# Feed-forward 2's weight splits moved into feed-forward 1, with DRAM copies; resident loads of w_out one by one; tiles reused in the last rows

## The chip, the cores and the metric

The kernel runs on one core of a Trainium2 chip. The metric is the device time of one execution in microseconds; three runs of the kernel before gave 1107.70, 1107.75 and 1108.04 us, median 1107.75 us.

## The reference, cut to what matters

Three stages follow one another: attention with a cumulative bias, a feed-forward with a cosine (feed-forward 1), and a normalised, gated feed-forward (feed-forward 2). B, H, S, D = 4, 8, 576, 64, so there are 2304 tokens of 512 features.

```python
scores = where(causal, -1e9, q @ k.T / sqrt(D) + minimum(-(cum_i - cum_j), 0))   # cum = cumsum(max(s, 0))
x  = (softmax(scores) @ v)  as [2304, 512]
h  = x @ w_in                     # [512, 2048]
x  = (h * cos(h)) @ w_out         # [2048, 512]
xn = x / sqrt(mean(x * x) + 1e-6) * rms_g
g, val = xn @ w_gate, xn @ w_val  # [512, 1536] each
out = (g * sigmoid(g) * val) @ w_out2        # [1536, 512]
```

The weights reach the chip as 64-bit words. Each product of the feed-forwards is made of three fp32r matmuls: both operands are split into a high part (`[:, 0]`) and a rest (`[:, 1]`), and high times high, high times rest and rest times high are summed in PSUM.

## The kernel before, in words

**A planner sets every order.** `Plan.op` (L90) collects operations with their alternatives (engine, cost in ns), a priority (`plan.now`, a due time) and what they read and write. `Plan.order` (L109) runs a list schedule over the five engines with cost formulas and writes the program in the order of the planned starts. On the chip each engine then works through its own list strictly in that order; what isn't ready holds up all that stands behind it on that engine. All DMAs are issued by SP, in SP's order.

**Weights.** `chunk` (L355) takes one chunk of 128 x 512 weights: a 512 KB DMA into `raw` (three buffers), one operation on ScalarE or GpSimd (`cv`, L361/L362), one on GpSimd (L365), two on VectorE (L366, L368), a copy for the high part (`copy`, L283) and a subtraction for the rest (`two`, L296). The result is a 512 KB tile.

**Feed-forward 1** goes over 9 blocks of 256 tokens, each in 8 ticks (72 ticks, `k = 8 j + m`, L732). A tick takes two chunks of `w_in`: 24 matmuls with 256 columns into a bank `h` (`gemm1`, L634), then a chain: ScalarE L744 (`u`), VectorE L297 (`u` minus `h`), ScalarE L746 (sine), VectorE L297 (times `h`), ScalarE copy L286 (`g`, high part), VectorE L297 (`g`, rest). Then come the 12 matmuls with 512 columns that add `g` times two chunks of `w_out` into the accumulators (`gemm2`, L640), placed behind the next tick's `gemm1`. There are three buffers each of `u` and `g`. The split `w_in` stays in 16 tiles `wi`. The split `w_out` is stored to DRAM as `wo_d`, read back through the 4 tiles `ws` for block 1, and from block 2 (`RES`) on kept in 16 tiles `wr`, which lie where attention's tiles were: `att_end` is the end of all attention operations. Ticks of the first blocks stand between attention's operations.

**Between the blocks** `rms_norm` (L691) copies the accumulators to `y`, squares them on ScalarE, runs 12 tiny VectorE operations and 2 scalings (L713); `rms_store` (L717) transposes on TensorE (L724), copies to `xo` and stores to `xn_d`.

**Feed-forward 2** goes over 6 blocks of 384 tokens, each in 12 units. A unit has 24 matmuls with 384 columns (`gemm1` on a gate and a value chunk) and 9 with 512 (`gemm2` on an output chunk). Its 36 weight chunks are split one after the other (L800 to L806): the first four into `ws`, the rest into `wi` and `wr` as feed-forward 1 gives those tiles back. So from tick 64 on (the last block of feed-forward 1) until unit 10 the splits of 32 chunks run beside the matmuls.

Of the kernel before, what the change touches and what calls it, by code (L numbers as in the profile page):

```python
# [10 lines left out]
F32 = mybir.dt.float32  # L11
# [11 lines left out]
BLK1 = 256  # L23
# [191 lines left out]
def attention_moe_moe(ctx, tc, q2, k2, vp, s, w_in, w_out, w_gate, w_val, w_out2, rms_g, out):  # L215
# [64 lines left out]
    def on(e, ns, fn):  # L280
        return [(e, ns, fn)]
# [20 lines left out]
    def load(o, i, nbytes, r, w, issue=475.0, **kw):  # L302
        return plan.op(on("SP", issue, lambda: sp.dma_start(out=o(), in_=i())), r, w, dma=nbytes, **kw)
# [48 lines left out]
    wo_d = [dbuf(f"wo_d{f}", [128, 2, 512]) for f in range(F1)]  # L352


    def chunk(src, w):  # L355
        raw, g = raw_r.new(), cv_r.new()
        load(raw, lambda: src.bitcast(I32).rearrange("p (c t) -> p c t", t=2), 1 << 19, [], [raw])
        top, low = (lambda: raw()[:, :, 1]), (lambda: raw()[:, :, 0])
        v = lambda: g().bitcast(I32)
        plan.op([  # L360
            ("POOL", pool1(512), lambda: pool.tensor_scalar(out=g(), in0=top().bitcast(F32), scalar1=2.0 ** -112, scalar2=1.0, op0=ALU.mult, op1=ALU.mult)),  # L361
            ("ACT", act_s(512), lambda: act.activation(g(), top().bitcast(F32), AF.Copy, scale=2.0 ** -112)),  # L362
        ], [raw], [g])
# [307 lines left out]
    def tick_at(k):  # L671
        return T_FF1 + k * P_FF1
# [7 lines left out]
        load(wo_d[f], lambda f=f: w2[0, f]().bitcast(F32), 1 << 19, [w2[0, f]], [wo_d[f]])  # L680
    for j in range(1, NB1):
        for f in range(F1):
            if j > RES:
                w2[j, f] = w2[RES, f]
                continue
            plan.now = tick_at(8 * j + f // 2) - 4000.0
            w = w2[j, f] = ws_r.new() if j < RES else wr_r.new(f)
            plan.op(on("SP", 475.0, lambda w=w, f=f: sp.dma_start(out=w().bitcast(F32), in_=wo_d[f]())), [wo_d[f]], [w], dma=1 << 19,
                    after=[att_end] if j == RES else ())

    def rms_norm(j, acc):  # L691
# [24 lines left out]

    def rms_store(j, ys):  # L717
        for k in (0, 2):
            tr, xo = h_bank(j + 1) if j < NB1 - 1 else bank.new(4), xo_r.new()

            def go(tr=tr, k=k):
                for i in range(2):
# [5 lines left out]
            load(lambda k=k: xn_d[j]()[:, k:k + 2, :], lambda xo=xo: xo().rearrange("p (k t) -> p k t", k=2), 1 << 18, [xo], [(xn_d[j], k)])  # L728

    acc = {}  # L730
    xs = {}
    for k in range(8 * NB1):  # L732
        j, m = divmod(k, 8)
        plan.now = tick_at(k) - 12000.0
        if m == 0:
            xs[j] = load_x1(j)
            acc[j] = [psb(f"acc{t}", (t,)) for t in range(2)]
        h, u, g = h_bank(j), u_r.new(), g_r.new()
        for i in range(2):
            plan.now = tick_at(k)  # L740
            w = w1[2 * m + i]
            plan.op(on("PE", 1440, lambda i=i, w=w, h=h, x=xs[j]: gemm1(h()[:, BLK1 * i:BLK1 * i + BLK1], w(), [b() for b in x], BLK1)), [w, *xs[j]], [h])
        plan.now = tick_at(k) - LEAD_E
        plan.op(on("ACT", act_p(512) + 93, lambda u=u, h=h: act.activation(u().bitcast(I32), h(), AF.Identity, bias=quarter)), [h], [u])  # L744
        two(u, lambda u=u: u().bitcast(I32), h, 512, [h], [u], psum=True)
# [14 lines left out]
            plan.now = tick_at(k) - LEAD_E  # L760
            rms_store(j - 1, ys)
    plan.now = tick_at(8 * NB1)
    rms_store(NB1 - 1, rms_norm(NB1 - 1, acc[NB1 - 1]))


    T_FF2 = tick_at(8 * NB1 + 1)
# [132 lines left out]
```

## Time and profile before

| | |
|---|---|
| three runs, median | 1107.75 us |
| the profiled execution | 1110.82 us, its span 1109.0 us |
| TensorE busy | 1080.4 us (97%) |
| VectorE, ScalarE, GpSimd busy | 547.1, 528.7, 187.1 us |
| mean granted TensorE clock | 0.992 |
| the chain that ended last | TensorE 80%, VectorE 9% |

TensorE is busy nearly throughout, so the numbers to look for are the stretches in which it isn't. On the timeline, feed-forward 1 runs alone from about 300 us; tick 64 starts at 587.40 us, and the first matmuls of feed-forward 2 at 640.34 us. PE is TensorE, DVE VectorE, ACT ScalarE, POOL GpSimd, SP the engine that issues DMAs. A matmul's end is modelled, so the pace is read from start to start.

### The profile page before, as it was taken

How to read it: one execution, taken by the hardware profiler on the slowest of the kernel's cores; microseconds unless marked ns; L12 is line 12 of the kernel's file. 1: busy time of each engine (PE TensorE's matmuls, PEld its weight loads, DVE VectorE, ACT ScalarE, POOL GpSimd, SP SyncE). 2: the span in 40 equal slices, each digit the busy share in tenths (PEclk: the TensorE clock that was granted, in tenths of full speed). 3: DMA queues.
4: the chain of work that ended last, by engine and by line, in shares of the span. 5: the costliest groups of instructions: out<-in, count | busy, mean ns of one | idle time of the engine just before them, and what ended most of it. 6: DMA issues, size and time to landing. Idle time of an engine off the chain costs nothing.

```text
span 1109.0 us, 16861 instructions
## 1 busy us (share of the span) xinstructions
PE 1080.4 (97%) x6474; PEld 938.8 (85%) x6474; DVE 547.1 (49%) x1209; ACT 528.7 (48%) x1098; POOL 187.1 (17%) x256
## 2 busy tenths in 40 slices
PE   8899999999999999999999999999999999999998
PEld 5568667777799999999998788999999999999997
DVE  6887998864474543535438888421211211211211
ACT  4889889988754543444435555321211211211111
POOL 3544556321030000000003444100000000000000
PEclk7999999999999999999999999999999999999999
DMA  5765677743392000000002537110000100100000
GB/s 179 239 205 172 212 252 234 241 142 107 123 390 65 22 27 20 20 29 30 20 20 80 164 120 223 39 57 1 25 34 1 57 1 1 43 1 1 30 1 29
DMA packets 51377, 101.28 MB, mean 91 GB/s; under 512 B 7520, under 2 KB 27488, under 8 KB 51296
## 3 DMA queue, kind: packets, MB, share of 16 engines
q1 hardware_dynamic: 51296, 100.19, 27.4%
q8 instruction: 51, 0.84, 0.3%
q14 instruction: 30, 0.25, 0.1%
HBM read 77.63 MB, written 22.54 MB: 90 GB/s over the span
## 4 chain that ended last, share of the span: by engine, by line
PE 80%; DVE 9%; issue 3%; POOL 3%; ACT 3%; DMA 1%; SPq 0%; DVEq 0%; POOLq 0%; ACTq 0%
PE bank L634 40%; PE bank L640 27%; PE bank L500 4%; PE bank L430 3%; PE bank L532 3%; DVE raw L366 2%; DVE cv L368 2%; POOL raw L365 1%; PE bank L457 1%; ACT cv L362 1%; DVE e L485 1%; PE bank L435 1%; DVE u L297 1%; DVE e L442 1%; PE bank L724 1%
## 5 line engine op out<-in xcount | busy, mean ns | idle before, releaser
L640 PE MATMUL bank<-wr,g 128*128 128x512 f32 x996 | 248.5, 396 | 4.7 <-ACT g L286 3.8
L297 DVE TENSOR_TENSOR u<-bank,u 128x512 f32<-128x512 f32 (+1 forms) x144 | 89.8, 623 | 313.0 <-PE bank L634 235.4
L634 PEld LDWEIGHTS bank<-xa,wi 128*128 128x128 f32 x1728 | 215.2, 188 | 9.1 <-DVE u L297 1.6
L634 PE MATMUL bank<-xa,wi 128*128 128x256 f32 x1728 | 221.3, 283 | 1.6 <-DVE u L297 1.4
L640 PEld LDWEIGHTS bank<-wr,g 128*128 128x128 f32 x996 | 182.6, 188 | 43.5 <-ACT g L286 4.9
L286 ACT ACTIVATE g<-u 128x512 fp32r<-128x512 f32 (+1 forms) x130 | 74.8, 576 | 265.2 <-DVE u L297 265.2
L297 DVE TENSOR_TENSOR g<-u,g 128x512 fp32r<-128x512 f32 (+1 forms) x127 | 82.4, 649 | 69.3 <-ACT g L286 69.2
L634 PE MATMUL bank<-xb,wi 128*128 128x384 f32 x528 | 101.8, 338 | 0.0
L634 PEld LDWEIGHTS bank<-xb,wi 128*128 128x128 f32 x528 | 93.7, 188 | 1.6
L634 PE MATMUL bank<-xb,wr 128*128 128x384 f32 x480 | 92.0, 335 | 0.0
L744 ACT ACTIVATE u<-bank,quarter 128x512 int32<-128x512 f32 x72 | 49.2, 684 | 81.0 <-PE bank L634 79.5
L297 DVE TENSOR_TENSOR u<-u,bank 128x512 f32<-128x512 int32 x72 | 49.3, 685 | 77.7 <-ACT u L744 76.2
L634 PEld LDWEIGHTS bank<-xb,wr 128*128 128x128 f32 x480 | 84.6, 188 | 1.8
L469 ACT ACTIVATE e<-e,mn 128x128 f32<-128x128 f32 (+3 forms) x128 | 70.6, 554 | 13.3 <-DVE mn L442 12.5
L746 ACT ACTIVATE u<-u,half_pi 128x512 f32<-128x512 f32 x72 | 52.1, 724 | 41.1 <-DVE u L297 40.8
L442 DVE CUSTOM_DVE_ANT_0 e<-bank,cm 128x128 f32<-128x128 f32 (+3 forms) x128 | 56.9, 484 | 22.9 <-PE bank L435 22.2
L640 PE MATMUL bank<-wi,g 128*128 128x512 f32 x270 | 66.8, 392 | 0.7 <-ACT g L286 0.7
L293 POOL TENSOR_SCALAR g<-u 128x512 fp32r<-128x512 f32 (+1 forms) x14 | 9.2, 659 | 340.6 <-DVE u L297 340.6
L826 ACT ACTIVATE u<-bank 128x384 f32<-128x384 f32 x72 | 35.2, 489 | 64.6 <-PE bank L634 53.2
L361 POOL TENSOR_SCALAR cv<-raw 128x512 f32<-128x512 f32 x20 | 15.0, 751 | 291.8 <-DVE wi L297 252.7
L640 PE MATMUL bank<-ws,g 128*128 128x512 f32 x246 | 64.0, 401 | 0.0
L365 POOL TENSOR_SCALAR raw<-raw 128x512 f32<-128x512 f32 x68 | 52.3, 770 | 68.0 <-ACT cv L362 65.6
(131 smaller groups left out, 1522.8 us busy)
## 6 DMA issues: line engine op xcount, KB each, us to landing
raw<-in_w_out_dram SPq DMA_DIRECT2D x28, 512.0 KB, 3.9
raw<-in_w_in_dram SPq DMA_DIRECT2D x16, 512.0 KB, 4.7
wo_d<-ws SPq DMA_DIRECT2D x16, 512.0 KB, 4.8
ws<-wo_d SPq DMA_DIRECT2D x16, 512.0 KB, 4.1
wr<-wo_d SPq DMA_DIRECT2D x16, 512.0 KB, 10.2
raw<-in_w_val_dram SPq DMA_DIRECT2D x12, 512.0 KB, 3.7
raw<-in_w_gate_dram SPq DMA_DIRECT2D x12, 512.0 KB, 3.7
qr<-in_q_dram SPq DMA_DIRECT2D x16, 320.0 KB, 4.8
```

The lines of the kernel that those rows point to most:

```text
L286: alts.append(("ACT", (act_p if psum else act_s)(n), lambda: act.activation(o(), i(), AF.Copy, scale=scale)))
L297: alts = on("DVE", dve1(n), lambda: dve.tensor_tensor(out=o(), in0=a(), in1=b(), op=op))
L365: plan.op(on("POOL", pool1(512), lambda: pool.tensor_scalar(out=top().bitcast(F32), in0=top().bitcast(F32), scalar1=0.0, scalar2=1.0, op0= ...
L430: pe.matmul(Sp[e]()[:, o:o + w], run.q()[hd, q0:q0 + 128], run.k()[hd, :w], start=(t == ts[0]), stop=False)
L442: plan.op(on("DVE", dve1(w) + 17, lambda o=o, w=w, i=i, e=e: dve.tensor_tensor_reduce(out=Es[e]()[:, o:o + w], in0=Sp[e]()[:, o:o + w], in ...
L469: plan.op(on("ACT", act_s(w) + 187, lambda E=E, o=o, w=w, i=i: act.activation(E()[:, o:o + w], E()[:, o:o + w], AF.Exp, scale=-1.0, bias=s ...
L500: pe.transpose(tr()[:m, 128 * j:128 * j + 128], E[0]()[:, E[2] + c:E[2] + c + m], ident)
L634: pe.matmul(h, w[:, a, 128 * k:128 * k + 128], x[k // 2][:, k % 2, c, :blk], start=(n == 0), stop=(n == 11))
L640: pe.matmul(acc[t], g[a][:, 128 * t:128 * t + 128], w[:, c, :], start=(first and (a, c) == (0, 0)), stop=(last and (a, c) == (1, 0)))
L744: plan.op(on("ACT", act_p(512) + 93, lambda u=u, h=h: act.activation(u().bitcast(I32), h(), AF.Identity, bias=quarter)), [h], [u])
L746: plan.op(on("ACT", act_s(512) + 93, lambda u=u: act.activation(u(), u(), AF.Sin, scale=-TWO_PI, bias=half_pi)), [], [u], table="sin")
L826: plan.op(on("ACT", act_p(BLK2), lambda us=us, h=hs[0]: act.activation(us(), h()[:, :BLK2], AF.Silu)), [hs[0]], [u], table="silu")
```

## The change

1. The 36 chunks of feed-forward 2's weights are split into the 4 `ws` tiles during ticks 24 to 64 of feed-forward 1: chunk n's raw load waits for the end of tick 24 + 40 n / 36. The first 32 are then stored to DRAM (`w3_d0` to `w3_d31`) and, where the split stood before, read back into the `wi` and `wr` tiles. The last four stay in `ws`.
2. The 16 loads of the resident `w_out` copies each wait, besides `att_end`, for the tick four ticks ahead of the one that uses them.
3. The normalisation of the last block gets a due time 20,000 ns later (`RMS_LATE`); the second half of each `rms_store` goes through `ys[0]` instead of `xo`; block 0 of feed-forward 2 uses four banks for `h` instead of five.

```diff
+RMS_LATE = 20000.0
+W3_FROM, W3_TO = 24, 64
-    def chunk(src, w):
+    def chunk(src, w, after=()):
-        load(raw, ..., 1 << 19, [], [raw])
+        load(raw, ..., 1 << 19, [], [raw], after=after)
     for j in range(1, NB1):
         for f in range(F1):
-            if j > RES:
-                w2[j, f] = w2[RES, f]
+            if j >= RES:
                 continue
...
-    def rms_norm(j, acc):
+    def rms_norm(j, acc, late=0.0):
...
+        plan.now += late
...
-            tr, xo = h_bank(j + 1) if j < NB1 - 1 else bank.new(4), xo_r.new()
+            tr, xo = h_bank(j + 1) if j < NB1 - 1 else bank.new(4), ys[0] if k else xo_r.new()
...
     for k in range(8 * NB1):
+        for f in (2 * m, 2 * m + 1):
+            if j == RES:
+                w2[j, f] = wr_r.new(f)
+                load(lambda f=f: w2[RES, f]().bitcast(F32), wo_d[f], 1 << 19, [wo_d[f]], [w2[j, f]], after=[att_end, ticks[k - 4]])
...
+            ticks[k] = plan.op(on("PE", 1440, ...gemm1...
...
-    rms_store(NB1 - 1, rms_norm(NB1 - 1, acc[NB1 - 1]))
+    rms_store(NB1 - 1, rms_norm(NB1 - 1, acc[NB1 - 1], RMS_LATE))
...
-        b = ws_r.new() if n < 4 else slots[n - 4][1].new(slots[n - 4][2])
-        w3[d, f] = chunk(w[f], b)
+    for n, (d, f, w) in enumerate(names):
+        plan.now = tick_at(8 * NB1)
+        b = chunk(w[f], ws_r.new(), [ticks[W3_FROM + n * (W3_TO - W3_FROM) // len(names)]])
+        if n < len(slots):
+            kept.append(dbuf(f"w3_d{n}", [128, 2, 512]))
+            load(kept[n], lambda b=b: b().bitcast(F32), 1 << 19, [b], [kept[n]])
+        else:
+            w3[d, f] = b
+    for n, (d, f, w) in enumerate(names[:len(slots)]):
...
+        b = w3[d, f] = slots[n][1].new(slots[n][2])
+        load(lambda b=b: b().bitcast(F32), kept[n], 1 << 19, [kept[n]], [b])
...
-            h = psb("h2", (6, 7, 2, 3, 4))
+            h = psb("h2", (6, 7, 2, 3, 4)) if j else psb("h2_0", (6, 7, 2, 3))
```

The order of the instructions changes in three places that matter here. Lines of the changed kernel are 2 to 19 higher (L297 is L299, L366 and L368 are L368 and L370).

VectorE in the middle of feed-forward 1, behind the normalisation of a block; before, these are two ticks:

```order
L297 TENSOR_TENSOR u_134<-u_134,bank_153 128x512
L297 TENSOR_TENSOR u_134<-bank_153,u_134 128x512
L297 TENSOR_TENSOR g_140<-u_134,g_140 128x512
L297 TENSOR_TENSOR u_135<-u_135,bank_151 128x512
L297 TENSOR_TENSOR u_135<-bank_151,u_135 128x512
L297 TENSOR_TENSOR g_141<-u_135,g_141 128x512
```

and in the changed kernel one tick:

```order
L299 TENSOR_TENSOR u_134<-u_134,bank_153 128x512
L368 SCALAR_TENSOR_TENSOR raw_129<-raw_129 128x512
L370 SCALAR_TENSOR_TENSOR cv_132<-cv_132,raw_129 128x512
L299 TENSOR_TENSOR u_134<-bank_153,u_134 128x512
L299 TENSOR_TENSOR ws_125<-cv_132,ws_125 128x512
L299 TENSOR_TENSOR g_140<-u_134,g_140 128x512
```

Each tick now holds three more VectorE operations: the two of the split (L368, L370) between the subtraction and the product, and the rest's subtraction (`ws`) between the product and `g`.

VectorE in ticks 65 and 66, where feed-forward 1 ends, before (`xc` are inputs of feed-forward 2, `st` the normalisation):

```order
L297 TENSOR_TENSOR u_135<-u_135,bank_151 128x512
L297 TENSOR_TENSOR wi_110<-cv_133,wi_110 128x512
L366 SCALAR_TENSOR_TENSOR raw_131<-raw_131 128x512
L297 TENSOR_TENSOR u_135<-bank_151,u_135 128x512
L368 SCALAR_TENSOR_TENSOR cv_132<-cv_132,raw_131 128x512
L366 SCALAR_TENSOR_TENSOR raw_129<-raw_129 128x512
L297 TENSOR_TENSOR g_141<-u_135,g_141 128x512
L368 SCALAR_TENSOR_TENSOR cv_133<-cv_133,raw_129 128x512
L297 TENSOR_TENSOR xc_5491<-xr_148,xc_5491 128x384
L289 CAST wi_112<-cv_133 128x512
```

and in the changed kernel:

```order
L299 TENSOR_TENSOR g_140<-u_134,g_140 128x512
L299 TENSOR_TENSOR xc_5768<-xr_148,xc_5768 128x384
L299 TENSOR_TENSOR u_135<-u_135,bank_151 128x512
L299 TENSOR_TENSOR u_135<-bank_151,u_135 128x512
L299 TENSOR_TENSOR g_141<-u_135,g_141 128x512
L706 TENSOR_SCALAR st_144<-st_144 128x2
L707 TENSOR_SCALAR st_144<-st_144 128x2
```

The splits into `wi_109` to `wi_112` and those of the next chunks are gone from here; the chain of the tick and the inputs of feed-forward 2 are left.

SP around the last block of feed-forward 1, before:

```order
L303 DMA raw_131<-in_w_gate_dram 128x1024
L303 DMA raw_129<-in_w_val_dram 128x1024
L303 DMA xr_148<-xn_d_221 128x256
L303 DMA xr_148<-xn_d_222 128x128
L303 DMA raw_130<-in_w_out_dram 128x1024
L303 DMA raw_131<-in_w_gate_dram 128x1024
L303 DMA raw_129<-in_w_val_dram 128x1024
L303 DMA raw_130<-in_w_out_dram 128x1024
L303 DMA raw_131<-in_w_gate_dram 128x1024
L303 DMA xn_d_228<-xo_139 128x512
L303 DMA raw_129<-in_w_val_dram 128x1024
```

and in the changed kernel (`w_d_246` is `w3_d0`, and so on):

```order
L305 DMA wi_109<-w_d_246 128x1024
L305 DMA wi_110<-w_d_247 128x1024
L305 DMA xr_148<-xn_d_221 128x256
L305 DMA xr_148<-xn_d_222 128x128
L305 DMA wi_111<-w_d_248 128x1024
L305 DMA wi_112<-w_d_249 128x1024
L305 DMA xr_148<-xn_d_221 128x256
L305 DMA wr_3067<-w_d_253 128x1024
L305 DMA xr_148<-xn_d_222 128x128
L305 DMA wr_3082<-w_d_255 128x1024
L305 DMA wi_113<-w_d_250 128x1024
L305 DMA wi_114<-w_d_251 128x1024
```

Where raw chunks were loaded, split tiles are read back; both are 512 KB each.

## Rows read from the trace of the kernel before

**Rows 1.** The page, parts 1 and 2: engine busy time, 40 slices.

```profile
PE 1080.4 (97%) x6474; PEld 938.8 (85%) x6474; DVE 547.1 (49%) x1209; ACT 528.7 (48%) x1098; POOL 187.1 (17%) x256
...
DVE  6887998864474543535438888421211211211211
...
PEclk7999999999999999999999999999999999999999
```

**Rows 2.** Windows: us, busy PE, PEld, DVE, ACT, POOL (x count), PEclk, DMA share, GB/s.

```profile
0.00:186.40 186.40, 171.89 (x1127) 123.67 (x1128) 154.80 (x428) 153.03 (x376) 91.88 (x137) 0.95 0.65 214
186.40:300.00 113.60, 113.22 (x809) 86.13 (x808) 71.84 (x229) 100.30 (x239) 25.49 (x44) 1.00 0.47 150
300.00:590.09 290.09, 290.09 (x1874) 263.73 (x1873) 138.69 (x260) 132.62 (x217) 9.34 (x10) 1.00 0.19 67
590.09:714.05 123.96, 115.09 (x636) 102.84 (x635) 102.20 (x159) 64.42 (x114) 50.75 (x55) 1.00 0.45 138
714.05:1109.00 394.95, 390.08 (x2035) 362.41 (x2033) 79.53 (x137) 78.38 (x154) 9.66 (x10) 1.00 0.06 20
306.50:320.60 14.10, 14.10 (x98) 13.05 (x97) 10.94 (x16) 8.54 (x14) 4.19 (x6) 1.00 1.02 405
```

**Rows 3.** Waits of PE, 590.09 to 714.05: waited for, us, times, longest.

```profile
PE bank L640 <- ACT g L286: 3.1, 4, 1.3
PE bank L724 <- DVE y L713: 2.6, 2, 1.9
PE bank L634 <- DVE u L297: 1.4, 1, 1.4
PE bank L634 <- ACT xo L286: 0.8, 1, 0.8
PE bank L640 <- DVE g L297: 0.8, 1, 0.8
```

**Rows 4.** Timeline, PE, feed-forward 1: start us, us, what.

```profile
382.86 1.03 PE L724 MATMUL bank<-ident,y 128*128 128x128 f32 x8
...
386.52 3.01 PE L634 MATMUL bank<-xa,wi 128*128 128x256 f32 x24
389.37 2.95 PE L640 MATMUL bank<-wr,g 128*128 128x512 f32 x12
392.17 3.02 PE L634 MATMUL bank<-xa,wi 128*128 128x256 f32 x24
```

**Rows 5.** Timeline, PE, feed-forward 2.

```profile
711.96 2.25 PE L640 MATMUL bank<-wr,g 128*128 128x512 f32 x9
714.05 1.23 PE L634 MATMUL bank<-xc,wr 128*128 128x384 f32 x6
...
718.24 2.02 PE L640 MATMUL bank<-wr,g 128*128 128x512 f32 x8
```

**Rows 6.** Timeline, one tick's chain at 447 us, all engines.

```profile
446.89 0.69 ACT L744 ACTIVATE u<-bank,quarter 128x512 int32<-128x512 f32 x1
...
449.82 0.63 ACT L286 ACTIVATE g<-u 128x512 fp32r<-128x512 f32 x1 [0.76 <-DVE u L297]
450.48 0.69 DVE L297 TENSOR_TENSOR g<-u,g 128x512 fp32r<-128x512 f32 x1 [0.70 <-ACT g L286]
...
452.25 2.95 PE L640 MATMUL bank<-wr,g 128*128 128x512 f32 x12
```

**Rows 7.** Timeline, GpSimd and VectorE side by side, tick 65.

```profile
595.36 1.60 POOL L299 TENSOR_TENSOR wi<-cv,wi 128x512 fp32r<-128x512 f32 x1
...
595.74 1.77 DVE L297 TENSOR_TENSOR g<-u,g 128x512 fp32r<-128x512 f32 x1
```

**Rows 8.** Groups of VectorE, 590.09 to 714.05.

```profile
L368 DVE SCALAR_TENSOR_TENSOR cv<-cv,raw 128x512 int32<-128x512 int32 x30 | 26.0, 868 | 0.8
```

**Rows 9.** Groups of GpSimd, 590 to 714.

```profile
L365 POOL TENSOR_SCALAR raw<-raw 128x512 f32<-128x512 f32 x30 | 24.4, 814 | 35.9 <-ACT cv L362 35.5
```

**Rows 10.** The page, part 6: DMA issues.

```profile
raw<-in_w_gate_dram SPq DMA_DIRECT2D x12, 512.0 KB, 3.7
```

More of the change, by code (lines that the diff above doesn't have):

```diff
@@ L352, in attention_moe_moe @@
     wo_d = [dbuf(f"wo_d{f}", [128, 2, 512]) for f in range(F1)]
-    def chunk(src, w):
+    def chunk(src, w, after=()):
         raw, g = raw_r.new(), cv_r.new()
-        load(raw, lambda: src.bitcast(I32).rearrange("p (c t) -> p c t", t=2), 1 << 19, [], [raw])
+        load(raw, lambda: src.bitcast(I32).rearrange("p (c t) -> p c t", t=2), 1 << 19, [], [raw], after=after)
         top, low = (lambda: raw()[:, :, 1]), (lambda: raw()[:, :, 0])
@@ L682, in attention_moe_moe @@
         for f in range(F1):
-            if j > RES:
-                w2[j, f] = w2[RES, f]
+            if j >= RES:
                 continue
             plan.now = tick_at(8 * j + f // 2) - 4000.0
-            w = w2[j, f] = ws_r.new() if j < RES else wr_r.new(f)
-            plan.op(on("SP", 475.0, lambda w=w, f=f: sp.dma_start(out=w().bitcast(F32), in_=wo_d[f]())), [wo_d[f]], [w], dma=1 << 19,
-                    after=[att_end] if j == RES else ())
-    def rms_norm(j, acc):
+            w = w2[j, f] = ws_r.new()
+            load(lambda w=w: w().bitcast(F32), wo_d[f], 1 << 19, [wo_d[f]], [w])
+    def rms_norm(j, acc, late=0.0):
         st, ys = st_r.new(), []
@@ L730, in attention_moe_moe @@
     acc = {}
-    xs = {}
+    xs, ticks = {}, {}
     for k in range(8 * NB1):
@@ L737, in attention_moe_moe @@
             acc[j] = [psb(f"acc{t}", (t,)) for t in range(2)]
+        for f in (2 * m, 2 * m + 1):
+            if j == RES:
+                w2[j, f] = wr_r.new(f)
+                load(lambda f=f: w2[RES, f]().bitcast(F32), wo_d[f], 1 << 19, [wo_d[f]], [w2[j, f]], after=[att_end, ticks[k - 4]])
+            elif j > RES:
+                w2[j, f] = w2[RES, f]
         h, u, g = h_bank(j), u_r.new(), g_r.new()
@@ L741, in attention_moe_moe @@
             w = w1[2 * m + i]
-            plan.op(on("PE", 1440, lambda i=i, w=w, h=h, x=xs[j]: gemm1(h()[:, BLK1 * i:BLK1 * i + BLK1], w(), [b() for b in x], BLK1)), [w, *xs[j]], [h])
+            ticks[k] = plan.op(on("PE", 1440, lambda i=i, w=w, h=h, x=xs[j]: gemm1(h()[:, BLK1 * i:BLK1 * i + BLK1], w(), [b() for b in x], BLK1)), [w, *xs[j]], [h])
         plan.now = tick_at(k) - LEAD_E
@@ L799, in attention_moe_moe @@
     w3, slots = {}, sorted([(f / 2, wi_r, f) for f in range(F1)] + [(f / 2 + WR_LATE, wr_r, f) for f in range(F1)], key=lambda v: v[0])
-    for n, (d, f, w) in enumerate((d, f, w) for f in range(F2) for d, w in (("g", w_gate), ("v", w_val), ("o", w_out2))):
+    names = [(d, f, w) for f in range(F2) for d, w in (("g", w_gate), ("v", w_val), ("o", w_out2))]
+    kept = []
+    for n, (d, f, w) in enumerate(names):
[7 more added lines that the diff above has]
+    for n, (d, f, w) in enumerate(names[:len(slots)]):
         if n == X0_AT:
```

## The prediction

> **What bounds the kernel now.** I read the page's busy times first, then windows by stage, then the waits of TensorE in the one stage that has many, and last the timeline there. The page says TensorE 97% busy at a granted clock that is full but for the start [rows 1]; so there is little to win, and the question is where the missing 28.6 us lie (1109.0 minus 1080.4). The windows answer it [rows 2]: 14.5 us up to 186.4 us (start and attention), 0.4 us up to 300 us, nothing at all in the 290 us of feed-forward 1 up to tick 65, 8.9 us between 590.09 and 714.05 us, 4.9 us behind that, the end included. The stretch with 8.9 us is the one in which feed-forward 2's weights are split: VectorE is 82% busy there (102.2 of 123.96) against 48% in feed-forward 1 (138.7 of 290.1), and TensorE waits there for results of VectorE and ScalarE, never for a DMA [rows 2, 3].
>
> Idle time understates the loss, since the array also refills behind each gap. I price the stretch by its work. The steady pace: 24 matmuls of 256 columns take 2.85 us (386.52 to 389.37) and 12 of 512 take 2.80 [rows 4]; 24 of 384 take 4.19 us (714.05 to 718.24) and 9 of 512 take 2.09 [rows 5]; 8 transposes 0.86 (382.86 to 386.52, less 2.80). In the window lie seven ticks' first products (65 to 71, 168 matmuls), nine ticks' second products (108), ten units' second products (90), ten and a half units' first products (252), 16 transposes, and two that straddle its start: 636, as its row counts [rows 2]. Work: 7 x 2.85 + 9 x 2.80 + 10 x 2.09 + 10.5 x 4.19 + 2 x 0.86 = 19.95 + 25.2 + 20.9 + 44.0 + 1.7 = 111.8 us. The stretch took 123.96, so 12.2 us are lost there. That is the most the change can bring.
>
> **The change part by part.**
>
> *The splits leave the stretch.* 30 splits start in it [rows 8]; each holds two VectorE operations at 0.87 and 0.80 us there, a subtraction and a GpSimd step of 0.81 [rows 9]. Gone with them is most of what VectorE does beside the chains: at 0.69 us alone [rows 6], 30 x 3 x 0.69 = 62 of its 102 us. What is late next is the last block's normalisation and the inputs of feed-forward 2, which stay. TensorE waited 2.6 us for that normalisation and 0.8 for its `xo` copy [rows 3]; both are now due later and meet a VectorE that is half free, but the tiny operations still stand in one run ahead of unit 1's product. I leave 1.5 us of the 12.2 there (bounds 0 and those 3.4). Gain 10.7.
>
> *The splits arrive in feed-forward 1.* 36 in 40 ticks, three VectorE operations in nearly every tick. VectorE load: 48% plus 36 x 3 x 0.69 = 75 us over 230 us (40 ticks of 5.65 and the transposes), some 80%. Whether TensorE feels it is decided by the chain of a tick: from ScalarE's first step at 446.89 to the end of the `g` copy at 450.45 it takes 3.56 us, and the matmuls that read `g` start only at 452.25 [rows 6], so 1.8 us are free. The two split operations stand between subtraction and product, where VectorE idles about 0.8 us for the sine: 2 x 0.69 - 0.8 adds 0.6. The GpSimd step can hold up one of them by its 0.81 [rows 9]. Together 1.4, under 1.8: an ordinary tick stays hidden. Ticks with a normalisation (five blocks) have the tiny operations and two scalings as well; I allow 0.4 us each, half of the last waits listed [rows 3], so 2.0 us. Bounds: nothing (as in the 290 us of feed-forward 1), or what a split costs in the stretch of before, 12.2 / 30 = 0.41 us, times 36 = 14.6. I take 2.0, nearer to nothing, because of the free 1.8 us.
>
> How far a GpSimd subtraction reaches shows in tick 65: VectorE's `g` took 1.77 us beside one [rows 7] and 0.69 alone [rows 6]. The Trainium skill (SBUF — State Buffer, section SBUF: two separate sides) says that a VectorE operation with two SBUF inputs and a GpSimd operation take a shared port pair in turn, and that the loser waits for the whole instruction; the trace agrees (1.08 us more). By that rule the five weight subtractions that the new order gives to GpSimd in feed-forward 1 could cost 0.6 + 0.81 + 1.08 - 1.8 = 0.7 us each, 3.5 us in place of 2.0.
>
> *The copies through DRAM.* 32 stores and 32 loads of 512 KB are added, 32 raw loads move. In feed-forward 1 the DMA engines are 19% busy [rows 2] and a raw load lands in 3.7 us [rows 10], less than a tick; the stores wait on nothing that a matmul needs. On SP a store that waits for its subtraction holds up the inputs `xr` of the next block behind it; these have the matmuls of a tick as cover, and I take nothing; where they came late the cause would be the same late VectorE, so the 14.6 above bounds this too. The reads back ask for four tiles a tick, 2.1 MB in 5.65 us or 371 GB/s, from tick 64 on; the 16 resident loads ran at 405 GB/s with TensorE fully busy [rows 2]. At that rate the 16.8 MB are there 41 us behind 590, at 631, and unit 0 starts near 632 with two tiles needed, the 32nd not until ten units later, at 632 + 10 x 6.28 = 695 (a unit is 4.19 + 2.09). Cost nothing; at the 138 GB/s that the stretch moved before they would take 122 us, to 712, which bounds the cost at 17 us.
>
> *Resident w_out one by one.* They made no wait before (no idle in 300 to 590) and have four ticks of lead: nothing either way.
>
> *Attention.* Two early splits leave it, behind 186 us; TensorE idles 0.4 us from there to 300. Gain at most 0.4, taken as nothing. The end (4.9 us with the tail) keeps its instructions. Four banks for `h` in block 0 are two units' worth, and a bank would be missed only if a unit's chain lasted longer than the next unit's 6.28 us; even the longer chain of a tick takes 3.56 [rows 6]: nothing; the second `xo` through `ys[0]` saves a wait for a store, inside the 1.5 above.
>
> Sum: -12.2 + 1.5 + 2.0 = -8.7 us. The profiled execution took 1110.82 us with a span of 1109.0, so 1102.1 for it; it lay 3.07 above the median of the three runs, and the forecast for the median is 1107.75 - 8.7 = 1099.0 us.
>
> **The rivals.**
>
> *Moved, not removed (slower).* The place is the chain of a tick in feed-forward 1, the price 0.41 us per split as in the stretch of before: +14.6 - 12.2 = +2.4, 1110.2 us. It decides once a split lengthens the chain by more than the free 1.8 us, or when a late raw chunk stops ScalarE, which now takes the first step of each split just ahead of the tick's own. For it: VectorE at some 80%, as busy as where the waits are now. Against it: the stretch holds a split every 4.1 us (123.96 / 30), feed-forward 1 will have one in 6.4 (230 / 36), with far fewer GpSimd subtractions and no inputs of feed-forward 2.
>
> *Half the gain stays away.* The normalisation and the inputs of feed-forward 2 keep their 3.4 us of waits, and feed-forward 1 loses about 1 us a block: -12.2 + 3.4 + 5 = -3.8, 1103.9 us. For it: the tiny operations are as many as before, in one run. Against it: VectorE ahead of them is free.
>
> *The reads back come late (slower).* At 138 GB/s the last tile is 17 us late: 1099.0 + 17 = 1116.0 us. For it: stores and loads share the DMA engines with the inputs of feed-forward 2. Against it: the 405 GB/s, and that below 160 GB/s alone anything is late (16.8 MB in the 105 us from 590 to 695).
>
> That the planner leaves the splits where they were is excluded: their raw loads wait for ticks 24 to 64.
>
> **How the numbers follow.** Chances: the forecast 0.70, half the gain 0.10, moved 0.12, late reads 0.03, and 0.05 for what lies between half the gain and moved, which is no change. About 0.2% (2.2 us) is what a measurement of this kernel can tell from no change: faster 0.80, same 0.05, slower 0.15. The range starts at 1095.2, the whole 12.2 and the 0.4 of attention, and reaches to 1106.5, past half the gain; 1110 stays outside. The predicted time is 1099.0.
>
> **What would show it.** TensorE busy without a gap in ticks 24 to 63 with VectorE near 80% there; ticks of 5.65 us; no waits for `g` behind 590 us; tick 64 at about 587 to 590 us and the first matmul of feed-forward 2 near 632. I am wrong if waits for `g` or `u` turn up at 360 to 590 us, if ScalarE stands at the first step of a split for a DMA, or if TensorE waits for the DMAs of the `wi` and `wr` tiles behind 630 us.

## The result and the profile after

The changed kernel takes 1097.32 us (median of four runs, 1096.32 to 1099.42) against 1107.89 us of the kernel before on the same chip: ratio 0.990, 95% interval 0.9885 to 0.9913. So it is 10.6 us faster; the forecast was 8.7 us, 1099.0. The profiled execution took 1099.42 us with a span of 1097.6, 11.4 us less than the span before.

The page of the changed kernel, parts 1 and 2, answers to [rows 1]:

```profile
PE 1077.4 (98%) x6474; PEld 938.8 (86%) x6474; DVE 538.8 (49%) x1219; ACT 535.3 (49%) x1108; POOL 162.8 (15%) x236
...
DVE  6888998754453777768677331221221211211211
...
PEclk7999999999999999999999999999999999999999
```
VectorE's row: from the fourteenth slice on (357 us) stood 3 to 5 tenths and then four 8s, the old splits; now nine slices have 6 to 8 (357 to 604 us), and two 3s follow. TensorE's busy time is 3.0 us less (1080.4 to 1077.4), the span 11.4: what went was mostly idle time.

The windows by stage answer to [rows 2]; the borders are the starts of tick 24 and of tick 64, one matmul at the end of feed-forward 2's first block (the second of its last value product), and the end. Columns as there.

```profile
357.23:588.48 231.25, 230.70 (x1481) 209.01 (x1480) 171.78 (x303) 140.35 (x237) 36.60 (x46) 1.00 0.53 179
588.48:709.41 120.93, 120.93 (x693) 111.85 (x692) 39.54 (x82) 38.16 (x70) 2.19 (x3) 1.00 0.45 162
709.41:1097.60 388.19, 383.31 (x2002) 356.15 (x2000) 78.35 (x135) 77.50 (x152) 9.68 (x10) 1.00 0.06 20
610.00:620.00 10.00, 10.00 (x72) 9.25 (x71) 3.45 (x5) 4.13 (x7) 0.00 (x0) 1.00 1.02 389
620.00:630.00 10.00, 10.00 (x64) 8.95 (x63) 3.61 (x6) 4.09 (x6) 0.00 (x0) 1.00 1.01 396
```
In the second row, where the kernel before had its 8.9 us of gaps, busy TensorE equals the stretch: there is none. The last two rows show the reads back: the DMA engines are full (share 1.01 and 1.02, 389 and 396 GB/s) and TensorE has no gap.

From mark to mark, with the same marks in the trace of before. There the first matmul of tick 64 starts at 587.24 us, not at 587.40 as written ahead of the prediction; the last mark but one is at 720.49:

| stretch | before | after | difference |
|---|---|---|---|
| start to tick 24 | 357.50 | 357.23 | -0.27 |
| ticks 24 to 63 | 229.74 | 231.25 | +1.51 |
| tick 64 to feed-forward 2's first matmul | 53.10 | 45.92 | -7.18 |
| block 0 of feed-forward 2, to its last value product | 80.15 | 75.01 | -5.14 |
| the rest | 388.51 | 388.19 | -0.32 |

The two stretches with the old splits give 12.32 us, and feed-forward 1 takes 1.51 of it back. The only waits of TensorE from 290 to 730 us, against the five groups of [rows 3]:

```profile
PE bank L642 <- ACT g L288: 0.5, 2, 0.3
```
Both lie in a tick behind a normalisation, and the blocks that hold them take 0.62 and 0.67 us more than before from transposes to transposes (46.59 and 46.61 against 45.97 and 45.94). So a wait of 0.27 us costs more than its recorded length; what is lost beyond it is called refill here, and no run takes it apart. The timeline of one of them, all engines, only the rows on the chain, answers to [rows 6]:

```profile
463.80 0.68 ACT L752 ACTIVATE u<-bank,quarter 128x512 int32<-128x512 f32 x1
...
464.90 1.41 DVE L714 SCALAR_TENSOR_TENSOR y<-y,st,gbc 128x512 f32<-128x512 f32 x2
...
466.23 0.68 DVE L299 TENSOR_TENSOR u<-u,bank 128x512 f32<-128x512 int32 x1
...
466.82 0.69 DVE L368 SCALAR_TENSOR_TENSOR raw<-raw 128x512 int32<-128x512 int32 x1
...
467.55 0.69 DVE L370 SCALAR_TENSOR_TENSOR cv<-cv,raw 128x512 int32<-128x512 int32 x1
468.15 0.68 DVE L299 TENSOR_TENSOR u<-bank,u 128x512 f32<-128x512 f32 x1
...
468.87 0.63 ACT L288 ACTIVATE g<-u 128x512 fp32r<-128x512 f32 x1
...
469.56 3.05 PE L642 MATMUL bank<-wr,g 128*128 128x512 f32 x12 [0.27 <-ACT g L288]
```
ScalarE's `u` is there at 464.48 (463.80 plus 0.68), but VectorE works in order: the tiny operations and the two scalings stand ahead, so the tick's subtraction starts at 466.23, 1.75 us late. With the split's two operations behind it `g` is late by 0.27 us for a `gemm2` that could have started at 469.3.

VectorE's groups of the splits in ticks 24 to 63 answer to [rows 8]:

```profile
L370 DVE SCALAR_TENSOR_TENSOR cv<-cv,raw 128x512 int32<-128x512 int32 x36 | 29.0, 806 | 0.4
...
L368 DVE SCALAR_TENSOR_TENSOR raw<-raw 128x512 int32<-128x512 int32 x36 | 24.9, 691 | 13.4 <-POOL raw L367 13.4
```
All 36 are there. GpSimd's groups of the same stretch answer to [rows 9]:

```profile
L367 POOL TENSOR_SCALAR raw<-raw 128x512 f32<-128x512 f32 x36 | 25.0, 695 | 244.6 <-ACT cv L364 238.2 <-DMA xr<-x_d_1a 4.9 <-DVE raw L368 1.5
L301 POOL TENSOR_TENSOR ws<-cv,ws 128x512 fp32r<-128x512 f32 x5 | 6.5, 1291 | 3.5 <-DVE ws L291 3.3
```
The second split operation takes 806 ns beside feed-forward 1's chains against 868 before, and GpSimd's step 695 against 814. Of the 36 subtractions GpSimd took five. VectorE's share is 74% (171.78 of 231.25), not the 80% of the forecast, against 46% before (104.70 us). The page's part 6, the reads back, answers to [rows 10]; the last column is the time to landing:

```profile
wi<-w_d SPq DMA_DIRECT2D x16, 512.0 KB, 5.3
wr<-w_d SPq DMA_DIRECT2D x16, 512.0 KB, 5.6
```
They take longer than the raw loads' 3.7 us, and nothing waits for them.

### The profile page after: what moved, and what is told of

The parts are those of the page before. It is cut to its first block, busy times and chain, and to the rows that moved or that the text cites. A ratio compares the mean times of both kernels' runs of the same rounds, so it can differ in the third digit from the quotient of the medians.

```text
span 1097.6 us, 17021 instructions
## 1 busy us (share of the span) xinstructions
PE 1077.4 (98%) x6474; PEld 938.8 (86%) x6474; DVE 538.8 (49%) x1219; ACT 535.3 (49%) x1108; POOL 162.8 (15%) x236
## 4 chain that ended last, share of the span: by engine, by line
PE 87%; DVE 7%; ACT 2%; issue 2%; POOL 2%; DMA 1%; DVEq 0%; POOLq 0%; ACTq 0%
PE bank L636 44%; PE bank L642 30%; PE bank L502 4%; PE bank L432 3%; PE bank L534 3%; DVE raw L368 1%; DVE cv L370 1%; PE bank L459 1%; DVE e L487 1%; PE bank L437 1%; PE bank L726 1%; DVE u L299 1%; DVE e L444 1%; DMA raw<-in_w_out_dram 0%; POOL raw L367 0%
## 5 line engine op out<-in xcount | busy, mean ns | idle before, releaser
L299 DVE TENSOR_TENSOR u<-bank,u 128x512 f32<-128x512 f32 (+1 forms) x144 | 89.7, 623 | 340.0 <-PE bank L636 268.4
L642 PE MATMUL bank<-wr,g 128*128 128x512 f32 x942 | 234.0, 396 | 0.5 <-ACT g L288 0.5
L642 PEld LDWEIGHTS bank<-wr,g 128*128 128x128 f32 x942 | 173.1, 188 | 35.4 <-ACT g L288 1.0
L299 DVE TENSOR_TENSOR g<-u,g 128x512 fp32r<-128x512 f32 (+1 forms) x132 | 84.8, 642 | 63.3 <-ACT g L288 61.8
L636 PE MATMUL bank<-xb,wr 128*128 128x384 f32 x528 | 101.0, 335 | 0.0
L636 PEld LDWEIGHTS bank<-xb,wr 128*128 128x128 f32 x528 | 93.1, 188 | 2.1
L367 POOL TENSOR_SCALAR raw<-raw 128x512 f32<-128x512 f32 x68 | 48.6, 715 | 256.1 <-ACT cv L364 247.9
L642 PE MATMUL bank<-ws,g 128*128 128x512 f32 x300 | 77.5, 399 | 1.3 <-ACT g L288 1.3
L299 DVE TENSOR_TENSOR u<-u,bank 128x512 f32<-128x512 int32 x72 | 49.3, 685 | 56.3 <-ACT u L752 55.2
L642 PEld LDWEIGHTS bank<-ws,g 128*128 128x128 f32 x300 | 54.0, 188 | 15.7 <-issue 3.1
```

The source lines that it names most:

```text
L299: alts = on("DVE", dve1(n), lambda: dve.tensor_tensor(out=o(), in0=a(), in1=b(), op=op))
L636: pe.matmul(h, w[:, a, 128 * k:128 * k + 128], x[k // 2][:, k % 2, c, :blk], start=(n == 0), stop=(n == 11))
L642: pe.matmul(acc[t], g[a][:, 128 * t:128 * t + 128], w[:, c, :], start=(first and (a, c) == (0, 0)), stop=(last and (a, c) == (1, 0)))
```

## The experiments

Profiled executions differ by up to 3 us in their first 60 us, where the granted clock is not yet full (0.79 to 0.91 in the first 20 us of the traces). So stages are compared from mark to mark. A mark that every kernel has is the transposes of a block; this table gives the four blocks of feed-forward 1 between the transposes near 382 us and those near 567 us.

| kernel | splits | median us | 95% of the ratio | transposes | four blocks |
|---|---|---|---|---|---|
| before | none here | 1107.89 | | 382.86, 566.67 | 183.81 |
| changed | 36 in 40 ticks | 1097.32 | 0.9885 to 0.9913 | 382.62, 567.87 | 185.25 |
| e4 | none | 1095.61 | 0.9866 to 0.9907 | 382.71, 566.52 | 183.81 |
| e5 | 36 in 40, weight subtractions not on GpSimd | 1097.27 | 0.9882 to 0.9914 | 383.02, 568.38 | 185.36 |
| e9 | 36 in 48 | 1112.50 | 1.0035 to 1.0060 | 379.72, 563.88 | 184.16 |
| e12 | 36 in 46 | 1096.79 | 0.9867 to 0.9900 | 382.67, 568.53 | 185.86 |
| e10 | 36 in 30 | 1105.05 | 0.9957 to 0.9984 | 384.43, 575.03 | 190.60 |
| e3 | 36 in 20 | 1112.68 | 1.0023 to 1.0052 | 380.67, 581.14 | 200.47 |

### Part 1 alone, parts 2 and 3 alone

```diff
 # e1: the changed kernel with parts 2 and 3 taken back
-            if j >= RES:
+            if j > RES:
+                w2[j, f] = w2[RES, f]
                 continue
...
-    rms_store(NB1 - 1, rms_norm(NB1 - 1, acc[NB1 - 1], RMS_LATE))
+    rms_store(NB1 - 1, rms_norm(NB1 - 1, acc[NB1 - 1]))
...
 # e2: the changed kernel with the old loop of splits in feed-forward 2
```

Expected of the splits alone: 

> The moved splits with their DRAM copies alone: the resident w_out loads go out together, the last normalisation is due as before, the second half of a block goes through xo, block 0 has five banks. Theory: the splits beside feed-forward 1's end were the whole loss of 12.2 us; with VectorE free there the normalisation is early enough by itself, so nearly all of the gain stays: 1097 to 1099.5 us, and TensorE waits under 1 us between tick 64 and unit 10. Rival (the small edits carry a part): the 2.6 us for the normalisation's y and the 0.8 us for xo stay as waits, 1100.5 to 1101.5 us.

Measured: 1100.94 us (ratio 0.9915 to 0.9954), 7.0 of the 10.6 us, outside the expected 1097 to 1099.5. The time is in the rival's range, but the missing part is not where the rival put it: between tick 64 and unit 10 TensorE has no wait. TensorE's timeline of e1 at the first use of the resident copies:

```profile
327.39 3.12 PE L636 MATMUL bank<-xa,wi 128*128 128x256 f32 x24 [1.65 <-DVE u L299]
...
332.36 7.99 PE L642 MATMUL bank<-wr,g 128*128 128x512 f32 x32 [0.45 <-ACT y L288]
```
In the changed kernel the first products with the resident copies stand earlier:

```profile
322.60 5.76 PE L642 MATMUL bank<-wr,g 128*128 128x512 f32 x24
```
From attention's last matmuls (292.05) to the transposes at 384.24 it takes 92.19 us; in the changed kernel 89.17 (293.45 to 382.62), with 581 matmuls in both. These 3.0 us are e1's loss; from the transposes to the end it takes 715.06 us, the changed kernel 714.98.

Expected of the rest alone: 

> All but the moved splits: w_out's resident loads one by one, the last normalisation due 20 us later, ys[0] for the second half, four banks in block 0; feed-forward 2's weights are split where they were. Theory: only the waits for the normalisation and its xo copy can go, 3.4 us at most, while the waits for g and u (5.3 us) stay: 1104.5 to 1107.5 us. Rival (the small edits carry a part, and the splits less): 1100 to 1104 us.

Measured: 1108.08 us, ratio 0.9986 to 1.0019: nothing. The waits in the old stretch stay, as TensorE's list from 586 to 720 us shows (columns as in [rows 3]):

```profile
PE bank L726 <- DVE y L714: 2.8, 2, 1.6
PE bank L642 <- ACT g L288: 2.7, 3, 1.4
PE bank L642 <- DVE g L299: 1.2, 2, 0.8
PE bank L636 <- DVE u L299: 0.3, 1, 0.3
```

### Which of the small edits counts once the splits have moved

```diff
 # e8: the changed kernel with part 3 taken back, part 2 kept
-    rms_store(NB1 - 1, rms_norm(NB1 - 1, acc[NB1 - 1], RMS_LATE))
+    rms_store(NB1 - 1, rms_norm(NB1 - 1, acc[NB1 - 1]))
-... ys[0] if k else xo_r.new()
+... xo_r.new()
-            h = psb("h2", (6, 7, 2, 3, 4)) if j else psb("h2_0", (6, 7, 2, 3))
+            h = psb("h2", (6, 7, 2, 3, 4))
 # e7: the changed kernel with
-RMS_LATE = 20000.0
+RMS_LATE = 0.0
```

> The changed kernel with part 3 undone: the splits in feed-forward 1 and the resident loads of w_out one by one, but the normalisation's due time, the second xo and the five banks as before. The splits alone gave 1100.9, and their trace loses time in one place only against the changed kernel: near 327 us, where block 2 begins, TensorE waits 1.65 us for u and 0.45 us for the copies of the accumulators, and 11 more matmuls than in the changed kernel's order stand ahead of the first that read the resident copies. Theory: the loads one by one take that away, part 3 is worth nothing: 1097.3 (1096.5 to 1098.3), no wait above 0.6 us between 300 and 340. Rival: the extra 3.6 us of the splits alone are the normalisation, the second xo and the banks of part 3: 1100 to 1101.5, with waits for y or xo between 590 and 720.

> The changed kernel with the last block's normalisation at its old due time. The prediction kept 1.5 us for waits of this normalisation and of the inputs of feed-forward 2; the changed kernel shows none of them. Theory: with the splits gone from these ticks VectorE is 33% busy, and the normalisation is no trouble at either place: 1097.3 (1096.5 to 1098.3). Rival: the later due time took them away: 1098.5 to 1100.5 here, with waits of 1 to 3 us for y or g between 600 and 670.

Measured: e8 1097.07 us (0.9883 to 0.9910), e7 1097.32 us (0.9884 to 0.9918). Both are the changed kernel's time, so part 3 is worth nothing, and the loads one by one are worth the 3.9 us between e1 and e8, though without the move (e2) they show nothing.

### What the splits still cost in feed-forward 1

```diff
 # e4 leaves feed-forward 2's splits out: it loads tiles of w_out's split in their place
-        b = chunk(w[f], ws_r.new(), [ticks[...]])
+        b = ws_r.new()
+        load(lambda b=b: b().bitcast(F32), wo_d[n % F1], 1 << 19, [wo_d[n % F1]], [b], after=[ticks[...]])
 # e5: the subtraction of these 36 splits on VectorE alone (psum=True leaves GpSimd out)
-        two(lambda: w()[:, 1, :], g, ..., 512, [g], [w])
+        two(lambda: w()[:, 1, :], g, ..., 512, [g], [w], psum=subs == ("DVE",))
...
+        b = chunk(w[f], ..., ("DVE",))
```

> The changed kernel with feed-forward 2's splits left out: each ws tile is loaded with a tile of split w_out from DRAM in place of a raw chunk, then stored and read back as before; feed-forward 2 so computes with other weights. It prices what the splits still cost in feed-forward 1. Theory: 1.35 us, the difference of ticks 24 to 64 between the two profiles: 1095.5 to 1096.5 us. Rival (the splits cost nothing there, the 1.35 us come from the added DMAs on SP's queue): within 0.4 us of the changed kernel, 1097 to 1097.7 us.

> The changed kernel, with the subtraction of each of the 36 moved splits on VectorE alone; GpSimd did 6 or fewer of them in feed-forward 1, at 1.29 us each. Theory: what is left of the splits' cost there (231.25 us for ticks 24 to 63, against 229.90 before, 1.35) lies in ticks behind a normalisation, where the chain itself is late, and not beside a GpSimd subtraction; so nothing changes: 1097.3, 1096.5 to 1098.2, ticks 24 to 63 in 231.0 to 231.6. Rival, the shared port: each GpSimd subtraction holds VectorE up by its length, 0.7 us for each of five by the prediction's working; without them 1.35 us at most come back: 1096.0, ticks 24 to 63 in 229.9 to 230.2.

Measured: e4 1095.61 us, four blocks in 183.81, the pace of before to the hundredth, and no wait of TensorE at all from 290 to 730 us. So 1.4 us of the splits are left, all of it their arithmetic, none the transfers'. e5: 1097.27 us, four blocks in 185.36 against 185.25. GpSimd's five weight subtractions cost nothing. But three subtractions for the input tiles `xa` stay on GpSimd in e5 as in the changed kernel, and e5's two waits stay too (0.23 and 0.28 us). In the tick ahead of the normalisation of each block that waits, one of the three runs beside the second operation of a split:

```profile
454.07 1.29 POOL L301 TENSOR_TENSOR xa<-xr,xa 128x512 fp32r<-128x512 f32 x1 [1.94 <-ACT xa L288]
454.11 1.80 DVE L370 SCALAR_TENSOR_TENSOR cv<-cv,raw 128x512 int32<-128x512 int32 x1
```
The operation takes 1.80 us there against 0.69 in the tick shown above (467.55); the third lies in a block without a wait. So e5 clears the weight subtractions only; what the `xa` subtractions cost was not tested.

### How close the splits may stand

```diff
 # e3, e10
-W3_FROM, W3_TO = 24, 64
+W3_FROM, W3_TO = 24, 44
+W3_FROM, W3_TO = 24, 54
```

> The splits in ticks 24 to 44 in place of 24 to 64, 1.8 a tick. Theory (a tick's chain has 1.8 us free, and what lengthens it further is lost by TensorE): two splits put up to four VectorE operations between the subtraction and the product, 4 x 0.69 - 0.8 = 2.0 us, and up to two GpSimd steps of 0.7, so 0.2 to 1.6 us over in each of some 20 ticks: 4 to 30 us more, 1101 to 1127 us, with waits for g and u in these ticks. Rival 1 (a fixed price per split, 0.41 us as in the stretch of before): 1097 + 13 = 1110 us however dense. Rival 2 (VectorE's load alone decides, and TensorE is hidden as long as VectorE is under 100%): within 2 us of the changed kernel.

> The changed kernel with the 36 splits in 30 ticks (24 to 54) in place of 40; in 20 ticks they cost 13.3 us more. Two theories of what sets that limit. The chain: a split adds 1.4 us to a tick's chain, of which 1.8 us are free, so one per tick is hidden and a second adds 1.0 us; six of the 30 ticks have two, so 6 us more, 1103.3 (1101 to 1105.5), with waits of TensorE for u or g of about 1 us in every fifth tick. The throughput: VectorE has 5.65 - 2.71 = 2.94 us free in a tick and a split takes 3 x 0.69 = 2.07, so 1.42 splits a tick fit and below that nothing is lost: 1097.3 to 1098.5 here. The 20 ticks do not tell these apart: 16 ticks with two splits make 16 us by the chain, and 20 x (2.71 + 1.8 x 2.07 - 5.65) = 15.7 us by the throughput.

Measured: e3 1112.68 us, e10 1105.05. e3 alone does not tell the theories apart; e10 does, since VectorE is only 76% busy in its four blocks (144.35 of 190.60 us; the changed kernel's 75%, 138.18 of 185.25), and yet they take 5.35 us more. So the throughput of the whole stretch (0 to 1.2 us) is not what decides. The time is near the chain's answer (6), but by luck, for the expected form was not right: the loss isn't 1 us in every fifth tick but four waits of 0.2 to 2.3 us with their refills, two of them within 13 us ahead of a block's transposes, where its normalisation runs. The timeline of e10 ahead of its longest wait:

```profile
463.06 1.60 POOL L301 TENSOR_TENSOR ws<-cv,ws 128x512 fp32r<-128x512 f32 x1
...
463.42 0.67 ACT L752 ACTIVATE u<-bank,quarter 128x512 int32<-128x512 f32 x1
463.44 1.25 DVE L706 TENSOR_SCALAR st<-st 128x2 f32<-128x2 f32 x1
...
466.00 0.68 DVE L299 TENSOR_TENSOR u<-u,bank 128x512 f32<-128x512 int32 x1
...
466.67 0.69 DVE L368 SCALAR_TENSOR_TENSOR raw<-raw 128x512 int32<-128x512 int32 x1
...
467.39 0.69 DVE L370 SCALAR_TENSOR_TENSOR cv<-cv,raw 128x512 int32<-128x512 int32 x1
468.00 0.68 DVE L299 TENSOR_TENSOR u<-bank,u 128x512 f32<-128x512 f32 x1
...
468.72 0.63 ACT L288 ACTIVATE g<-u 128x512 fp32r<-128x512 f32 x1
...
469.40 2.98 PE L642 MATMUL bank<-wr,g 128*128 128x512 f32 x9 [2.27 <-ACT g L288]
```
ScalarE's `u` is there at 464.09, but the subtraction starts only at 466.00; two operations of a split stand between it and the product, and the tiny operations of the normalisation between all of them: `gemm2` comes 2.27 us late. The first tiny operation takes 1.25 us beside a subtraction of GpSimd, 0.17 us in e5. e10 gives 12 weight subtractions to GpSimd, e3 24, the changed kernel 5. And VectorE is 89% busy from 455 to 470 us (13.39 of 15.00). So in these ticks the order of the chain, GpSimd's subtractions and a VectorE that is nearly full come together, and no run separates them.

### The reads back

```diff
 # e6: a copy of each kept tile from DRAM to DRAM, beside the reads
         b = w3[d, f] = slots[n][1].new(slots[n][2])
+        more = dbuf(f"more{n}", [128, 2, 512])
+        load(more, kept[n], 1 << 19, [kept[n]], [more], after=[ticks[64 + n // 4]])
```

> The changed kernel with a copy of 512 KB from DRAM to DRAM added for each of the 32 tiles read back, beside the reads in ticks 64 to 71: twice the bytes for the DMA engines, whose share is 0.98 to 1.02 from 600 to 630 us already. Theory: the reads come early enough to give away half their pace: at half of 390 GB/s the 16.8 MB take 86 us from 590, to 676, and the last tile is needed at about 689; 1097.3 to 1099. Rival, the reads are barely in time: a tile of the first units comes late, and each microsecond shows; 1105 or more, with waits for the DMAs of wi or wr between 630 and 690.

Measured: 1098.29 us (0.9895 to 0.9927), at most some 1.0 us more. Windows of e6 (columns as above):

```profile
600.00:610.00 10.00, 10.00 (x64) 8.95 (x63) 4.48 (x8) 4.50 (x7) 0.00 (x0) 1.00 1.01 385
...
650.00:660.00 10.00, 10.00 (x54) 9.24 (x53) 4.25 (x17) 3.58 (x9) 0.00 (x0) 1.00 1.04 427
660.00:670.00 10.00, 10.00 (x53) 8.81 (x52) 0.99 (x2) 1.69 (x3) 0.00 (x0) 1.00 1.01 421
```
The DMA engines are full from 600 to 670 us, in the changed kernel to 630; a read of `wi` lands in 9.6 us in place of 5.3, and no matmul waits for one (TensorE's only new wait is 1.2 us for `u`).

### Spreading the splits further

```diff
 # e9, e12
-W3_FROM, W3_TO = 24, 64
+W3_FROM, W3_TO = 24, 72
+W3_FROM, W3_TO = 18, 64
```

> The changed kernel with the splits spread over ticks 24 to 72 in place of 64, three for every four ticks. What the splits still cost in feed-forward 1 is 1.35 us, in the ticks behind a normalisation (no splits at all: 1095.6). By the chain and by the throughput alike, fewer of these ticks have a split: 1096.0 to 1097.3, the two waits for g of 0.27 us gone or one left. Against it: the last splits fall beside the last block's normalisation and the reads back, where the kernel before lost its 12.2 us; if eight splits there bring back a quarter of that, 1100.3, with waits for u, y or g between 600 and 670.

Measured: 1112.50 us, slower than the kernel before. Feed-forward 1 did as expected (184.16), then the timeline of TensorE shows this:

```profile
631.56 3.36 PE L642 MATMUL bank<-wr,g 128*128 128x512 f32 x12 [0.92 <-ACT g L288]
640.86 0.47 PE L726 MATMUL bank<-ident,y 128*128 128x128 f32 x1 [5.93 <-DVE y L714]
...
643.93 2.27 PE L636 MATMUL bank<-xc,wi 128*128 128x384 f32 x6
646.00 1.10 PE L636 MATMUL bank<-xb,wi 128*128 128x384 f32 x3
```
With the second product of tick 71 done at about 634.9, TensorE is empty until the normalisation is through. In the changed kernel the first units of feed-forward 2 stand ahead of these transposes:

```profile
634.40 1.22 PE L636 MATMUL bank<-xc,wi 128*128 128x384 f32 x6
635.46 1.22 PE L636 MATMUL bank<-xb,wi 128*128 128x384 f32 x6
...
653.99 0.60 PE L726 MATMUL bank<-ident,y 128*128 128x128 f32 x4
```
There the transposes come 20 us behind the first unit's start, and the whole normalisation lies beside matmuls. In e9 the units could not stand ahead: one quarter of their input goes through a `cv` tile, which the last splits still held; its load was issued only at 644.39 (583.78 in the changed kernel):

```profile
643.67 0.69 DVE L299 TENSOR_TENSOR ws<-cv,ws 128x512 fp32r<-128x512 f32 x1 [0.81 <-ACT ws L288]
...
644.39 0.79 SPq L305 DMA_DIRECT2D cv<-xn_d  x2
```
One run puts that load late without touching the splits:

```diff
 # e11
+    ys_last = rms_norm(NB1 - 1, acc[NB1 - 1], RMS_LATE)
...
-                         ..., [(xn_d[b], k0)], [(raw, c0)])
+                         ..., [(xn_d[b], k0)] + ([ys_last[1]] if (j, k) == (0, 3) else []), [(raw, c0)])
```

> The changed kernel, its splits in ticks 24 to 64 as they are; only the load of one input tile of feed-forward 2 (the fourth quarter of block 0's x2, which goes through a cv tile) waits until the last block's normalisation has scaled y. This asks why the splits spread to tick 72 made 1112.5 us: there that load waited for the cv tile of the last splits, was issued at 644.39, the planner put the last transposes ahead of feed-forward 2's first unit, and TensorE stood empty for 5.93 us with a clock of 0.51 to 0.79 for the 16 us behind it. Theory, the late input alone does that: from the transposes of tick 64 to the end the wider spread took 500.84 us against 483.76, 17 us more, so 1112 to 1115 here, with a gap of about 6 us ahead of the last transposes and a granted clock below 0.9 behind it. Rival, the splits beside the normalisation and the reads did it: without them 1097.3 to 1100, full clock.

> The changed kernel with the splits spread over ticks 18 to 64 in place of 24 to 64, so that the cv tile is free when it was. With the wider spread ticks 24 to 63 took 230.14 us against 231.22, so the splits' cost there fell from 1.35 to about 0.3. Theory: the same here, 1096.0 to 1097.2, waits for g behind a normalisation one or none. Rival: the early splits meet the 16 resident loads of w_out (405 GB/s near tick 16) and the first use of these tiles, where the splits alone lost 2 us to waits: 1098.5 to 1101, with waits between 310 and 350.

Measured: e11 1110.91 us (1.0002 to 1.0029), a little under the theory's range from 1112 on and far above the rival's, with the order of e9, a gap of 5.46 us and half the clock behind it. From the transposes near 612 us to the end: changed kernel 483.76 us, e9 500.84, e11 498.83. So one late quarter of an input costs 15 us, and by difference the splits of e9 beside the normalisation and the reads 2. Windows of e11 behind the gap:

```profile
636.00:640.00 4.00, 0.00 (x0) 0.00 (x0) 1.55 (x10) 2.08 (x6) 0.00 (x0) 0.89 0.93 317
640.00:644.00 4.00, 1.75 (x6) 1.06 (x7) 1.82 (x5) 0.60 (x1) 0.00 (x0) 0.50 0.11 38
644.00:648.00 4.00, 4.00 (x15) 4.00 (x14) 1.03 (x2) 1.42 (x3) 0.00 (x0) 0.50 0.42 156
...
656.00:660.00 4.00, 4.00 (x14) 3.46 (x13) 0.00 (x0) 0.00 (x0) 0.00 (x0) 0.57 0.00 0
```
e12 made 1096.79 us, the expected time, but not for the expected reason: its four blocks took 185.86, not less than 185.25, with three waits for `g` of 0.3 us in place of one or none. So thinner spread is not what removes the rest. No kernel that does the same work beat the changed one measurably.

## Why the prediction was right

**The loss in the old stretch, 12.2 us, was there to take.** The two stretches gave 12.32. Pricing the stretch by its work, and not by its 8.9 us of idle time, made the sum: the other 3.4 us are lost beyond the recorded idle time. e1 shows that the splits' move is what takes it: behind the transposes at 382 us it is the changed kernel to 0.1 us.

**The 1.5 us left to the last normalisation and to the inputs were 0.** The step said that the tiny operations "still stand in one run ahead of unit 1's product". They do run there, but TensorE has units of feed-forward 2 to work on meanwhile. The due time is not the cause (e7, e8).

**Feed-forward 1, 2.0 us, measured 1.51.** The working by the chain held for the ordinary ticks: 1.8 us free against 1.4 added, and TensorE waits in none of them. Five ticks behind a normalisation at 0.4 us were allowed; two lost some 0.65 us each, with waits of 0.27. So the sum is near, but its form is partly luck. At 1.2 splits a tick the slack is gone (e10), at VectorE 76% busy. The four blocks without split work (e4) show that nothing else costs there. Two of the named signs of being wrong showed in small: these waits for `g`, and ScalarE at a split's first step for its raw chunk, three times, 1.0 us in all; the raw chunks held up no matmul.

These two terms are most of the error in size: 1.5 + 0.5 us, with 0.6 in the stretches priced at nothing and 0.1 in the 12.2, are the 2.7 us between -8.7 and the -11.4 of the spans.

**The shared port.** GpSimd's subtractions lengthen single operations of VectorE, as [rows 7] showed, but without the five for weights the four blocks took 0.1 us more (e5), so the second price, 3.5 us, was wrong. The Trainium skill (SBUF — State Buffer, section SBUF: two separate sides) says that a VectorE operation with two SBUF inputs and a GpSimd operation that reads SBUF take turns. The rows agree on the length of one operation (1.77 us in [rows 7], 1.80 in e5). The five subtractions for weights cost nothing; whether the port is part of the loss where the slack is short, behind the normalisations and in e10 and e3, was not tested.

**Copies and reads, nothing.** Right, and with a margin: e6 doubles the traffic for 1.0 us. The bound of 17 us (138 GB/s) had been the demand of the stretch before and not what the DMA engines can do: 389 and 396 GB/s in the changed kernel.

**Resident w_out one by one, "nothing either way".** This step was wrong, though the sum did not suffer. The reason given was that they made no wait before; with the splits moved the planner writes another order, and there the loads in one go cost 3.0 us at block 2 (e1). TensorE's two waits there are for `u` and `y`, not for a load; that the order makes them is read from e1's timeline and not tested by itself. A price read from the order of before doesn't hold for the order after.

**The rivals.** "Moved, not removed" took 0.41 us for any split; the measured price is 0.05 us at 36 in 40 ticks (185.25 less 183.81, by the 29 splits between these transposes), but 0.54 at 36 in 20 (e3: 200.47 less 183.81, by 31). So the rival described a denser spread. "Half the gain" fell with the changed kernel's trace, which has no wait for the normalisation, and e7 and e8 show that the later due time isn't the reason; "late reads" fell with e6. The rival that could have turned the sign was not among them: one input tile late behind the splits (e9, e11), 15 us.

What stays open: why e12 gained nothing in feed-forward 1 where e9 gained 1.1 us. The traces give a hint. Three splits in four ticks fall alike on every block of eight: in e9 the tick ahead of the normalisation, 24 to 18 us before the transposes, holds no split in any of the five blocks, and GpSimd has no subtraction in ticks 24 to 63. In the blocks that wait, two of the changed kernel and two of e12, that tick holds one. But blocks without a wait hold one there too (transposes at 428.71 and 567.87 in the changed kernel, 474.68 in e12), and no run moves that split alone. Open too is what part of e11's 15 us is the half clock alone (its added waits are 5.46 + 0.91 + 1.97 + 0.9, the rest 5.8 us).

## What to carry to other kernels

Price a stretch by its instructions at the steady pace, then ask of the work moved whether it fits the slack of the tightest ticks, not the average share of an engine: here 0.9 splits a tick cost 1.4 us and 1.2 cost 7 more with the engine three quarters busy. Before work is spread further, look at the tiles it holds: the last splits of e9 kept the tile that one input needs, so its load went out at 644.39 us in place of 583.78, and with it went the matmuls that had covered the normalisation. And price side edits in the new order: the same loads were worth nothing alone and 3.9 us together with the move.

## What the runs showed of the hardware

Behind 5.46 us of empty TensorE the granted clock was 0.50 from 640 to 648 us (e11), one of the two levels, 1.2 GHz; behind 5.93 us it was 0.51 from 640 to 644 us (e9). In e9 six matmuls of 384 columns took 2.07 us there, from their start to that of the next six (643.93 to 646.00); at the full clock they take 1.06 (634.40 to 635.46 in the changed kernel). In e11 it was 1.00 again from 652 to 656 us and fell once more, to 0.57 from 656 to 660, behind a wait of 1.97 us. The DMA engines moved 385 to 427 GB/s from 600 to 670 us (e6) without one gap in TensorE's work. And a VectorE operation that starts beside a GpSimd subtraction took 1.80 us in place of 0.69 (e5).
